# A four-layer attention and bilinear-MLP kernel whose instruction orders and PSUM banks are exchanged for another set

## The chip, the cores and the metric

The kernel runs on one core of one Trainium2 chip. The metric is the device time of one execution in microseconds (us), the median of several runs; lower is better. Engine names are those of the profile: PE is the matrix engine's matmuls, PEld its weight loads, DVE the vector engine, ACT the scalar engine, POOL the GpSimd engine, SP the SyncE queue that issues nearly all DMAs here.

## What is computed

Two sub-layers, A (sliding, dilated local attention) and B (a bilinear gated MLP), each behind a layernorm and with a residual, run twice on one sequence of 2048 tokens with 448 features.

```python
def _A_ref(x, wqkv, wo):              # H = 16 heads of 28
    W, dil = 8, 2                     # 8 keys, every second position back
    q, k, v = ...                     # x @ wqkv, split by heads
    idx = pos[:, None] - off[None, :]
    logits = jnp.einsum("bhsd,bhswd->bhsw", q, kg) * scale
    attn = _softmax(jnp.where(mask, logits, -1e9), axis=-1)
    o = jnp.einsum("bhsw,bhswd->bhsd", attn, vg)
    return o.reshape(B, S, D) @ wo
def _B_ref(x, w_gate, w_up, w_down):  # F = 1792
    return ((x @ w_gate) * (x @ w_up)) @ w_down
x = x + _A_ref(_layernorm(x), A_wqkv, A_wo)
x = x + _B_ref(_layernorm(x), B_w_gate, B_w_up, B_w_down)
x = x + _A_ref(_layernorm(x), A_wqkv, A_wo)
x = x + _B_ref(_layernorm(x), B_w_gate, B_w_up, B_w_down)
```

## The kernel before, in words

**Layers and chunks.** The layers are numbered 0 (A), 1 (B), 2 (A), 3 (B). Each is cut into chunks of 256 or 512 tokens, and the chunks of neighbouring layers are interleaved. The building code appends every piece of work to one list (`Sched.add`); its place in the list is its number, from 0 to 1669, and these numbers are how this document names operations. An operation is one or several instructions of one engine with the results it needs (`deps`) and, for matmuls, the PSUM banks it takes (`acquire`) and who frees them (`release`).

**An A chunk.** DVE and ACT compute the layernorm of each block of 128 tokens: statistics (L583, L585), the inverse deviation by Ln and Exp (L586, L588), the normalised block xn (L604). xn is transposed into xnT: for layer 0 by PE and a copy out of PSUM (L614, L618, L628), for the other layers by a DMA that transposes (L607), which is operation ("T", layer, block). Queries and keys are matmuls over WQK (halves of one unit on PE), copied to qk by ACT or DVE (L714). V is a matmul copied to v_sb by ACT or DVE (L806, L779); in layers 0 and 2 the last four heads of most query blocks take another way: spare columns of WQK make them beside the queries and keys, DMAs copy them to memory (L723, tile vt) and a transposing DMA, the reload, brings them back (L734, ("VT", layer, block)). Scores (L837) are bursts of small matmuls in 32-column tiles, and in the first six groups of layer 0 in 64-column tiles. Exp runs on ACT (L847), the mask on DVE (L854). The product with V (L872) is another burst; two copies to O_sb (L886, ACT or DVE) and an addition (L890) follow, then the division through Ln and Exp (L900 to L913), which leaves oT. In layer 2 small DMAs, the moves, regroup oT so that its fourth chunk is half as long (L445, oT<-oT; ("mv", ...) and after them ("mw", ...)); a like regrouping of wo_g is loaded once (("wf", ...)). The output projection takes oT and wo_g, and DVE adds it to x_sb (L943).

**A B chunk.** 14 units of 128 features each: 14 matmuls (seven pairs over the two halves of the rows of PE, L352) make gate and up; ACT copies gate to g_sb (L979), DVE multiplies it with up into hT (L982). The down projection then takes hT and WD, and DVE adds to x_sb. The blocks of the last layer go out by DMA.

**What sets the order.** The order on every engine is written out by hand as a list of numbers, `ORDER["pe"]`, `["act"]`, `["dve"]`, `["pool"]`, `["sp"]` (from L104). Where an operation may run on ACT, DVE or POOL, the list it stands in decides. An entry of PE like `801+802+785*848/6/1` is a merged burst: the small matmuls of 801, 802 and 785 are spread between steps of the unit 848, of which six steps run as eight strips of 32 columns each (L355); the last number says how many whole steps go ahead. `BANKS` gives each matmul operation its PSUM banks. `schedule` (L227) expands the lists, and derives the waits for banks from the order; `emit` (L276) writes each engine's instructions with semaphore waits for what has not been waited for yet. Each engine, and the DMA queue of SP, works its list strictly in order.

**Operations that the text speaks of.** 47 to 62 are warm-up matmuls without use for the result; 63 to 70 copy the loaded query and key weights into WQK (L522, by DVE, ACT or POOL); 71 to 78 copy the four heads' columns (L530); 45 and 46 write qmask (L509, L510); 211, 212, 271, 272, 532 and 533 are halves of the score bursts of the groups 0, 2 and 5 of layer 0. 279 and 280 are the two copies to O_sb of group 2; 245 is a copy of V, 373 a smaller one; 362, 512, 588 and 590 copy queries and keys. 301 and 303 are transposes for the first B chunk. 776 and 777 are reloads for the query blocks 1 and 2 of layer 2; 801, 802, 785 and 786 their bursts with V; 917 is a transpose for the second A chunk of layer 2, whose query/key units begin with 922 or 928; 819 loads a part of the regrouped wo_g, which 823 finishes and 824 uses. 1229 is the last move ahead of 1230, the first half of the output projection of the blocks 8 and 9 of layer 2. 855 to 890, 1037 to 1060 and 1254 to 1293 are gate/up units and their copies.

Of the kernel before, what the change touches and what calls it, by code (L numbers as in the profile page):

```python
# [96 lines left out]
def grp_nc(g):  # L97
# [22 lines left out]
    ),  # L120
    "act": (
# [1003 lines left out]
```

## Time and profile before

| what | value |
|---|---|
| runs | 383.13, 384.85, 381.83 us; median 383.13 |
| profiled execution, its own time | 383.47 us |
| its span, first to last instruction | 381.7 us |
| granted PE clock | 1.000 |
| instructions of PE | 6388 matmuls, 6388 weight loads |

The profile shows one execution. The span is what the trace covers; 1.8 us of the execution's own time lie around it. Busy time of PE is from the start of a matmul to a modelled end, and matmuls overlap: two that use different halves of the rows run side by side, so a step's real cost is read from the start of one to the start of the next. Line numbers are those of the kernel; L352 and L355 are helpers that nearly all matmuls share, so the tiles tell them apart. "Idle before <-releaser" names what the profile takes to have ended an engine's idle time; where the named one has nothing to do with the instruction, it was another.

### The profile page before, as it was taken

To read this page: it belongs to the slowest core of one execution; us is meant where nothing else is said; L and a number is where in the kernel's file an instruction comes from. 1 tells how busy PE (TensorE), PEld (TensorE's weight loads), DVE (VectorE), ACT (ScalarE), POOL (GpSimd) and SP (SyncE) were. 2 spreads that over 40 slices of the span, in tenths; PEclk is the share of its full clock that TensorE was granted. 3 is DMA by queue.
4 is the path that set the end of the run, shared out by engine and by line. 5 is a ranking of instruction groups with operands and counts; after the bars stand their busy time and mean duration, and the time that the engine had idled before them with its cause. 6 is when DMAs were issued, how large, how long until landed. Compare 5 with 4: busy or idle time off the path is not lost.

```text
span 381.7 us, 14424 instructions
## 1 busy us (share of the span) xinstructions
PE 373.9 (98%) x6388; PEld 209.8 (55%) x6388; DVE 288.1 (75%) x649; ACT 198.0 (52%) x379; POOL 7.8 (2%) x36
## 2 busy tenths in 40 slices
PE   7999999999999999999999999999989999999997
PEld 3645577654554445444676666555555544444864
DVE  7988999989759794968568977758887878266423
ACT  5798896766516355245645326628745633034410
POOL 7000000000000000000000000000000000000000
PEclk9999999999999999999999999999999999999999
DMA  7665543500130215332102221630124001502003
GB/s 262 165 158 147 96 127 81 97 7 3 26 78 16 43 25 72 43 43 44 34 18 27 45 50 29 106 47 6 25 43 76 9 19 29 122 17 47 2 2 120
DMA packets 56209, 22.97 MB, mean 60 GB/s; under 512 B 45812, under 2 KB 56132, under 8 KB 56148
## 3 DMA queue, kind: packets, MB, share of 16 engines
q1 hardware_dynamic: 56004, 22.00, 27.5%
q8 instruction: 50, 0.82, 0.9%
q14 instruction: 11, 0.09, 0.1%
q10 hardware_dynamic: 144, 0.06, 0.1%
HBM read 8.59 MB, written 2.71 MB: 30 GB/s over the span
## 4 chain that ended last, share of the span: by engine, by line
PE 91%; DVE 4%; ACT 2%; DMA 1%; issue 1%; SPq 0%; DVEq 0%
PE ps L352 82%; PE ps L355 4%; PE ps L837 2%; PE ps L872 2%; PE ps L994 1%; ACT qk L714 1%; DMA v_sb<-vt 1%; DVE xn_sb L604 1%; DVE st L583 1%; DMA x_sb<-in_A_x_dram 1%; DVE v_sb L806 0%; DVE WQK L522 0%; DVE hT L982 0%; DVE Qz L825 0%; DVE xnTa L628 0%
## 5 line engine op out<-in xcount | busy, mean ns | idle before, releaser
L352 PE MATMUL ps<-xnTb,WGU 64*128 64x512 bf16 (+1 forms) x1890 | 171.2, 332 | 0.3 <-DVE qk L714 0.3
L352 PEld LDWEIGHTS ps<-xnTb,WGU 64*128 64x128 bf16 x1890 | 92.3, 94 | 70.6 <-issue 1.6
L979 ACT ACTIVATE g_sb<-ps 128x512 bf16<-128x512 f32 (+1 forms) x140 | 69.3, 510 | 83.9 <-PE ps L352 72.0
L982 DVE TENSOR_TENSOR hT<-g_sb,ps 128x512 bf16<-128x512 bf16 (+1 forms) x140 | 78.0, 574 | 36.3 <-ACT g_sb L979 35.5
L352 PE MATMUL ps<-WD,hT 64*128 64x448 bf16 x794 | 81.3, 349 | 0.0
L352 PEld LDWEIGHTS ps<-WD,hT 64*128 64x128 bf16 x794 | 38.3, 94 | 33.3 <-ACT E_sb L847 0.4
L943 DVE TENSOR_TENSOR x_sb<-x_sb,ps 128x448 bf16<-128x448 bf16 x62 | 37.1, 613 | 21.6 <-PE ps L352 21.3
L352 PE MATMUL ps<-xnTa,WQK 64*128 64x512 bf16 (+1 forms) x490 | 51.8, 352 | 0.3 <-DVE WQK L522 0.2
L847 ACT ACTIVATE E_sb<-ps,shift_sb 128x1024 bf16<-128x1024 f32 (+1 forms) x36 | 37.5, 1072 | 12.0 <-PE ps L837 11.9
L583 DVE BATCH_NORM_STATS2 st<-x_sb 128x6 f32<-128x448 bf16 x64 | 38.3, 613 | 1.0 <-DMA x_sb<-in_A_x_dram 0.8
L604 DVE TENSOR_SCALAR xn_sb<-x_sb,mv,rstd 128x512 bf16<-128x512 bf16 (+1 forms) x64 | 35.4, 574 | 2.5 <-ACT rstd L588 2.0
L352 PEld LDWEIGHTS ps<-xnTa,WQK 64*128 64x128 bf16 x490 | 23.0, 94 | 20.7 <-DVE O_sb L890 0.4
L714 ACT ACTIVATE qk<-ps 128x1024 bf16<-128x1024 f32 (+1 forms) x29 | 26.6, 931 | 11.4 <-PE ps L352 6.3
L901 ACT ACTIVATE R_sb<-R_sb 128x480 f32<-128x480 f32 (+1 forms) x34 | 20.4, 604 | 17.2 <-DVE R_sb L900 17.0
L854 DVE TENSOR_TENSOR E_sb<-E_sb,MK 128x1024 bf16<-128x1024 bf16 (+1 forms) x36 | 23.5, 656 | 6.6 <-ACT E_sb L847 6.6
L352 PE MATMUL ps<-wo_g,oT 64*128 64x448 bf16 x236 | 27.1, 349 | 1.1 <-DVE hT L982 1.1
L913 DVE TENSOR_TENSOR oT<-O_sb,R_sb 128x480 bf16<-128x480 f32 (+3 forms) x36 | 21.9, 626 | 3.8 <-ACT R_sb L902 3.6
L352 PE MATMUL ps<-WV,xnTa 64*128 64x336 bf16 (+3 forms) x248 | 23.2, 304 | 0.5 <-DVE O_sb L890 0.5
L900 DVE STREAM_SHUFFLE R_sb<-O_sb 128x480 f32<-128x480 f32 (+1 forms) x34 | 23.1, 692 | 0.0
L586 ACT ACTIVATE lnv<-mv,eps_sb 128x2 f32<-128x2 f32 (+2 forms) x31 | 9.0, 295 | 25.9 <-DVE mv L585 24.0
L902 ACT ACTIVATE R_sb<-R_sb 128x480 f32<-128x480 f32 (+1 forms) x34 | 20.0, 607 | 0.3
L886 ACT ACTIVATE O_sb<-ps 128x512 f32<-128x512 f32 (+1 forms) x20 | 10.9, 570 | 15.8 <-PE ps L872 15.8
(66 smaller groups left out, 223.8 us busy)
## 6 DMA issues: line engine op xcount, KB each, us to landing
out_dram<-x_sb SPq DMA_DIRECT2D x15, 112.0 KB, 1.8
x_sb<-in_A_x_dram SPq DMA_DIRECT2D x3, 448.0 KB, 5.3
hT<-in_A_wqkv_dram SPq DMA_DIRECT2D x4, 224.0 KB, 4.4
WGU<-in_B_w_gate_dram SPq DMA_DIRECT2D x4, 224.0 KB, 3.9
WGU<-in_B_w_up_dram SPq DMA_DIRECT2D x4, 224.0 KB, 4.5
WD<-in_B_w_down_dram SPq DMA_DIRECT2D x2, 448.0 KB, 3.8
WGU<-in_B_w_gate_dram SPq DMA_DIRECT2D x2, 336.0 KB, 4.5
WGU<-in_B_w_up_dram SPq DMA_DIRECT2D x2, 336.0 KB, 4.8
```

The costliest lines, as they stand in the source:

```text
L352: return lambda E: E.matmul(out(), lhs(), rhs(), start=start, stop=stop)
L583: sc.add("dve", one(lambda E, B=B: E.bn_stats(st6[:, B, :], x_sb[:, B, :]), ("bn", li, B)), 525.0, deps=[("x", li - 1, B)] + ([("xn", li - ...
L604: sc.add("dve", one(lambda E, B=B, dst=dst, src=src: E.tensor_scalar(dst, src, mv[:, B, 0:1], rstd[:, B:B + 1], ALU.subtract, ALU.mult), ( ...
L714: return E.activation(dst, src, ACT.Copy) if hasattr(E, "activation") else E.tensor_copy(dst, src)
L847: return E.activation(E_sb[:, slot, 2 * hp:2 * hp + 2, 0:w], ps[:, b0:b0 + 2, 0:w], ACT.Exp, bias=shift_sb[:, 0:1], scale=SCALE)
L854: return E.tensor_tensor(e, e, MK[:, kind, 0:nc].unsqueeze(1).unsqueeze(1).to_broadcast([128, 2, w // nc, nc]), ALU.min)
L900: sc.add("dve", one(lambda E: E.stream_shuffle(R_sb[:, rs, 0:w], O_sb[:, os_, 0:w], [DH] * 32), ("Rs", li, qb)), dve_est(w) + 20.0, deps=[ ...
L901: sc.add("act", one(lambda E: E.activation(R_sb[:, rs, 0:w], R_sb[:, rs, 0:w], ACT.Ln), ("Rl", li, qb)), act_est(w, False), deps=[("Rs", l ...
L913: return E.tensor_tensor(oT[:, :, a % HALF:a % HALF + z - a], O[:, :, a - tok:z - tok], R_sb[:, rs, 0:w].rearrange("p (h n) -> p h n", h=4 ...
L943: sc.add("dve", one(lambda E: E.tensor_tensor(x_sb[:, B, :], x_sb[:, B, :], ps[:, bk[w], 0:D], ALU.add), ("x", li, B)), dve_est(D), deps=[ ...
L979: sc.add("act", one(lambda E, gs=gs, bk=bk: E.activation(g_sb[:, gs, 0:nt], ps[:, bk[0], 0:nt], ACT.Copy), ("G", li, j, fc)), act_est(nt), ...
L982: sc.add("dve", one(lambda E, gs=gs, bk=bk, fc=fc: E.tensor_tensor(hT[:, fc, hs, 0:nt], g_sb[:, gs, 0:nt], ps[:, bk[1], 0:nt], ALU.mult), ...
```

## The change

All five orders and the table of banks are replaced; nothing else in the file differs. The 1670 operations are the same, and so are their shapes and the data that each needs. The new lists were searched with every transpose, move, copy and reload assumed to land late, and the initial loads ("fetches") left as they were. By comparison of the lists: 42 operations change engine, so that ACT has 383 entries for 379 and DVE 588 for 592; 68 steps of merged bursts run as strips instead of 69; the first loads stand in the same order on SP. The score bursts 211/212, 271/272 and 532/533 stood directly behind each other, and now other matmuls stand between their halves. 45 and 46 move to the front of DVE's list, POOL copies 65 and 64 in the place of 67 and 64, and makes masks after them.

The core of the diff, with the lines that the text speaks of:

```diff
     "pe": (
-        "47 48 49 50 51 52 53 54 55 112 56 57 58 109 59 60 61 127 62 130 206 238 207 136 239 133 194 198 195 199 232 200 233 196 201 226 197 227 228 155 149 229 "
-        "230 158 152 231 171 189 211 212 356 192 174 357 180 354 247 248 177 355 502 217 218 503 352 253 353 585 581 254 582 586 504 506 242 505 507 243 266 371 "
-        "267 271 272 372 358 508 359 509 277 583 278 584 381 382 375 579 376 405 580 406 387 307 310 388 313 319 322 304 290 316 291 328 340 532 533 334 331 325 "
-        "337 343 400 521 401 411 522 412 346 526 347 527 348 538+539+556*349/5/1 424 598 425 599 454 451 448 557+562*457/2/5 463 563+609*551/2/2 552 466 610 460 "
...
-        "801+802+785+786*863/5/2 727 875 857 922 866 923 887 924 926 925 927 941 869 928 878 946 942 929 881 1019 947 1022 1028 952 953 860 1031 872 1040 1043 "
...
-        "1367+1368*1284/4/2 1287 1201 1396 1202 1356 1290 1357 1351 1230 1352 1231 1397+1373+1374*1293/7 1296 1304 1297 1305 1361 1402+1403*1306/4 1362 1298 "
-        "1425+1426*1299/4/3 1307 1479 1473 1482 1476 1431+1432*1485/7 1494 1488 1491 1500 1420 1391 1421 1392 1512 1497 1503 1506 1509 1515 1523 1524 1449 1525 "
...
+        "47 48 49 50 51 52 53 54 55 56 57 112 58 59 60 109 61 62 127 206 130 207 133 238 239 136 194 200 195 201 232 198 233 226 196 199 155 197 227 158 230 228 "
+        "149 152 229 231 211 171 212 189 356 174 192 357 177 180 354 247 248 355 502 217 218 503 352 253 353 581 254 585 582 586 242 506 504 243 505 507 266 271 "
+        "267 371 272 358 508 372 359 509 583 277 584 278 381 382 375 376 579 405 580 406 307 304 387 313 388 310 316 319 322 290 328 291 532 334 340 325 533 411 "
+        "331 412 343 400 337 401 521 526 522 346 347 527 348 538+539+556*349/5/1 424 598 425 599 454 451 562+557*448/3 457 551 563 552 463 469 609+610*475/2 460 "
...
+        "712 773 752 706 756 774 757 750 715 754 753 751 697 755 709 652 779 780 653 769 718 795+796*719/2/5 770 720 721 724 725 854 726 851 801+802+785*848/6/1 "
+        "786 727 863 857 875 869 866 928 887 929 926 922 927 924 923 925 946 881 941 947 952+953*942/3/1 878 1022 1019 860 1031 1034 1028 1040 872 824 981 "
+        "958+959*825/3 1052 884 1043 1025 982*890/1/3 891 1046 987+988*896/2/5 892 1037 893 1049 897 1055 898 1083 1058 899 1077 1080 1061 976 1062 1089 1092 "
...
+        "1206+1207*1120/1/6+1171/1 1121 1257 1254 1172 1122 1260 1266 1332 1269 1338 1183+1184+1212+1213*1333/4+1339/3 1272 1336 1334 1337 1335 1281 1263 "
+        "1367+1368*1278/4/3 1290 1275 1396 1201 1351 1202 1352 1284 1356 1287 1230 1357 1231 1397+1373+1374*1293/7 1304 1361 1296 1402+1403*1297/5/2 1362 1298 "
...
     "act": (
-        "14 106 107 102 103 118 119 110 113 124 125 131 68 208 137 209 240 202 241 204 237 146 147 205 203 186 168 234 187 169 150 235 153 236 213 214 193 362 "
-        "249 250 361 510 223 224 256 255 588 263 259 264 260 511 512 244 273 274 374 298 299 363 513 280 279 589 383 384 287 407 408 308 283 311 284 288 314 320 "
...
+        "14 106 107 102 103 118 113 119 110 124 125 66 131 208 134 209 137 240 241 202 146 147 205 237 156 204 203 234 168 169 186 187 150 235 213 214 236 178 "
+        "249 250 361 219 510 223 224 255 256 590 263 264 259 260 244 511 245 273 274 298 299 373 374 363 513 589 280 384 383 407 408 308 283 284 305 287 314 288 "
...
     "dve": (
-        "15 17 104 105 16 100 111 101 114 116 108 117 115 120 122 126 129 123 121 128 65 66 45 135 140 132 63 70 69 138 134 139 160 144 161 142 182 143 164 162 "
...
-        "221 222 252 360 225 257 262 258 590 265 261 270 245 268 269 294 373 295 296 297 275 276 302 380 300 281 404 286 385 377 587 282 386 531 409 309 312 285 "
...
+        "15 17 45 46 104 105 16 100 111 101 116 114 108 115 117 122 120 126 121 123 129 128 132 140 135 68 63 67 70 69 141 138 144 142 139 145 162 143 182 154 "
+        "163 148 160 164 166 157 165 184 159 151 167 161 210 183 185 179 173 188 170 153 72 76 73 74 172 77 191 190 176 175 193 246 181 362 215 216 270 251 220 "
+        "221 222 252 360 225 257 262 258 265 588 261 512 268 269 294 296 295 297 275 302 300 276 380 279 404 281 282 377 385 386 409 587 286 531 309 306 285 315 "
...
     "pool": (
-        "21 24 25 32 26 23 35 39 33 36 18 34 28 44 20 37 29 40 19 30 38 27 41 31 42 43 22 67 64 71 78 73"
+        "24 22 25 32 23 35 26 44 20 28 29 27 30 18 19 36 21 65 64 39 33 31 40 75 41 78 71 42 34 37 43 38"
...
     "sp": (
...
-        "379 378 519 524 99 595 525 529 597 594 596 530 593 441 443 591 445 592 447 606 601 602 671 673 669 607 675 743 749 745 747 843 767 845 764 768 766 762 "
-        "841 847 763 765 772 776 917 819 777 915 919 921 1016 1018 816 817 815 814 935 820 821 934 822 938 939 936 818 823 937 940 945 944 950 949 1076 1074 973 "
...
+        "378 519 518 379 99 593 595 591 529 594 596 443 525 441 447 592 445 597 530 607 602 606 601 671 673 675 669 745 749 743 747 845 843 766 768 820 762 765 "
+        "767 764 763 841 847 772 776 777 917 915 919 921 822 819 821 1018 1016 944 938 940 939 823 814 816 817 934 937 815 935 936 818 945 949 950 1140 1074 "
...
 BANKS = (
-        "47:0 109:1 112:2 127:45 130:23 133:23 136:01 149:01 152:45 155:45 158:01 171:45 174:01 177:67 180:45 189:23 192:23 194:01 196:45 198:67 200:01 206:67 "
...
+        "47:0 109:1 112:2 127:45 130:01 133:23 136:01 149:01 152:67 155:01 158:01 171:67 174:23 177:23 180:45 189:67 192:67 194:67 196:23 198:45 200:23 206:67 "
```

101 rows, old and new, of tables (BANKS, ORDER) are left out of this document.

## The prediction

> **What bounds the kernel now.** I read the page first, then the waits of PE, then the busy time by stretch, then the timeline at each place where PE waits. From the page, the span and the busy time by engine:
>
> ```profile
> span 381.7 us, 14424 instructions
> PE 373.9 (98%) x6388; PEld 209.8 (55%) x6388; DVE 288.1 (75%) x649; ACT 198.0 (52%) x379; POOL 7.8 (2%) x36
> ```
>
> PE is busy for 373.9 of 381.7 us, and no other engine passes 75%. So 7.8 us of PE idle time is all that another order can remove, and only orders change here. The waits of PE over the whole span say where it lies (total, times, longest):
>
> ```profile
> PE ps L514 <- DVE hT L475: 1.3, 1, 1.3
> PE ps L352 <- DVE hT L982: 1.1, 1, 1.1
> PE ps L614 <- DVE xn_sb L604: 0.7, 2, 0.4
> PE ps L872 <- DMA v_sb<-vt: 0.5, 1, 0.5
> PE ps L352 <- DVE O_sb L890: 0.5, 1, 0.5
> PE ps L618 <- DVE xn_sb L604: 0.5, 1, 0.5
> PE ps L352 <- DVE qk L714: 0.3, 1, 0.3
> ```
>
> L514, L614 and L618 belong to the start (warm-up and transposes); after it PE idles four times, 2.4 us in all. The stretches agree (us, then busy time of PE, PEld, DVE, ACT and POOL, the granted clock, DMA share, GB/s):
>
> ```profile
> 0.00:24.00 24.00, 21.09 (x288) 11.31 (x290) 21.68 (x76) 16.96 (x38) 7.82 (x36) 1.00 0.73 206
> 24.00:60.00 36.00, 35.17 (x780) 21.41 (x777) 32.14 (x75) 31.57 (x53) 0.00 (x0) 1.00 0.51 119
> ```
>
> 2.9 us are idle before 24 us, 0.8 between 24 and 60, and in this second stretch DVE is busy for 32.14 of 36 us.
>
> **The change part by part.** No operation is added or removed. The sum is made against the profiled execution's 383.47 us; the median of the runs shown is 383.13, 0.34 lower, and they spread over 3.0.
>
> *Reload at 162 us.* PE, then SyncE:
>
> ```profile
> 161.62 0.40 PE L355 MATMUL ps<-xnTb,WGU 64*32 64x512 bf16 x8
> 161.89 0.40 PE L355 MATMUL ps<-xnTb,WGU 64*32 64x512 bf16 x8
> 162.82 0.25 PE L872 MATMUL ps<-E_sb,v_sb 64*32 64x64 bf16 x16 [0.53 <-DMA v_sb<-vt]
> 162.89 0.40 PE L355 MATMUL ps<-xnTb,WGU 64*32 64x512 bf16 x8
> ```
> ```profile
> 157.47 1.26 SPq L607 DMA_TRANSPOSE xnTa<-xn_sb  x1
> 158.83 0.42 SPq L445 DMA_DIRECT2D wo_g<-in_A_wo_dram  x1
> 159.30 2.36 SPq L734 DMA_TRANSPOSE v_sb<-vt  x1
> ```
>
> One step of such a burst follows the other after 0.27 us (161.62 to 161.89); here it took 1.00, so 0.73 is lost. Operation 802 wanted reload 777, which SyncE issued at 159.30 and which PE had 3.5 us later. In the new SP order 777 stands straight behind 776, ahead of transpose 917 (1.26) and the load 819 (0.42): it goes out 1.7 us earlier. That covers 0.73: **-0.73** (bounds -0.73 and 0). Transpose 917 goes back by one reload, about 1.2 us; it feeds a query/key chunk that PE began (922) two gate/up units after the burst (875, 857) and now begins (928) after five (863, 857, 875, 869, 866), and the load 819 serves only 824, far behind that. I cost both at nothing; without that cover they cost what the reload takes, 1.3 us at most.
>
> *Move at 277 us.* PE, SyncE, DVE:
>
> ```profile
> 274.01 0.59 PE L352 MATMUL ps<-WV,xnTa 64*128 64x336 bf16 x6
> 274.44 1.67 PE L352 MATMUL ps<-xnTb,WGU 64*128 64x512 bf16 x14
> 275.95 1.16 PE L352 MATMUL ps<-WV,xnTa 64*128 64x336 bf16 x14
> 278.25 0.93 PE L352 MATMUL ps<-wo_g,oT 64*128 64x448 bf16 x8 [1.14 <-DVE hT L982]
> ```
> ```profile
> 274.73 0.54 SPq L445 DMA_DIRECT2D oT<-oT  x1
> ```
> ```profile
> 274.62 1.14 DVE L943 TENSOR_TENSOR x_sb<-x_sb,ps 128x448 bf16<-128x448 bf16 x2
> ```
>
> Three pairs of 64x336 take 274.01 to 274.44, 0.143 each; seven from 275.95 end at 276.95. The next matmul, 1230, starts at 278.25, so 1.3 us are lost. The profile names hT, but 1230 reads no hT: it needs the two PSUM banks that the x additions of 274.62 freed by 275.76, and the move 1229 (oT<-oT, 274.73). The move is what is left, 3.5 us from issue to use. In the new PE order, after the same scores burst, 1290, 1275, 1396, 1201, 1351, 1202, 1352, 1284, 1356 and 1287 stand ahead of 1230, before it was 1287, 1201, 1396, 1202, 1356, 1290, 1357, 1351: two more gate/up units of 1.51 us (274.44 to 275.95) with the V halves unchanged, some 3.0 us more cover for 1.3 us of lateness: **-1.3** (bounds -1.3 and 0). The Trainium skill, "DMA: Bandwidth & Descriptors", section "Anatomy of one DMA", puts a DMA's fixed cost at about 2.0 us (for issues from GpSimd). By that the move is there at 276.7 and the wait has another cause; the trace has 3.5 us from issue to use. By the Trainium skill's figure the sum would be without the -1.3, and it is a rival below.
>
> *The first 24 us.* DVE, PEld and POOL:
>
> ```profile
> 8.68 0.81 DVE L522 COPY WQK<-hT 128x448 bf16<-128x448 bf16 x2
> 9.43 0.63 DVE L604 TENSOR_SCALAR xn_sb<-x_sb,mv,rstd 128x512 bf16<-128x512 bf16 x1
> 10.83 0.64 DVE L522 COPY WQK<-hT 128x448 bf16<-128x448 bf16 x3
> 18.10 0.37 DVE L510 MEMSET qmask<- 28x1 f32 x4
> ```
> ```profile
> 8.69 1.22 POOL L522 COPY WQK<-hT 128x448 bf16<-128x448 bf16 x2 [1.92 <-DMA hT<-in_A_wqkv_dram]
> ```
> ```profile
> 21.22 0.41 PEld L618 LDWEIGHTS ps<-ident,xn_sb 64*128 64x128 bf16 x16 [0.44 <-DVE xn_sb L604]
> 22.11 0.14 PEld L837 LDWEIGHTS ps<-Qz,qk 64*64 64x64 bf16 x8 [0.28 <-DVE xnTa L628]
> ```
>
> Three copies alone take 0.64, two beside POOL's copies 0.81, so POOL holds DVE up by about 0.4 there. The new order still gives POOL two copies (65 and 64 for 67 and 64), but 65 can start with an earlier load; DVE runs five in one row. DVE's mask writes (0.37, from 18.10) go to the gap before the first input lands. I take **-0.7**, the 0.37 and half of the two waits of 0.28 and 0.44; bounds 0 (DVE is held up again) and -1.1 (0.37 and both waits). The 16 warm-up matmuls are the same number, two of them now fill the first wait for xn.
>
> *Split scores visits.* In the early groups the scores run in another array tiling, which PE enters and leaves:
>
> ```profile
> 38.08 0.92 PE L352 MATMUL ps<-wo_g,oT 64*128 64x448 bf16 x8
> 38.92 0.64 PE L837 MATMUL ps<-Qz,qk 64*64 64x128 bf16 x32
> 39.50 0.74 PE L352 MATMUL ps<-WV,xnTa 64*128 64x448 bf16 x6
> ```
> ```profile
> 47.46 0.42 PE L837 MATMUL ps<-Qz,qk 64*64 64x128 bf16 x16
> 47.81 0.61 PE L352 MATMUL ps<-xnTa,WQK 64*128 64x256 bf16 x8
> ```
>
> A visit of 32 holds the queue for 0.58 us, one of 16 for 0.35: two halves cost 0.12 more, and the entry about 0.08 (38.08 to 38.92, less four pairs of 0.19). The new order splits three visits (211/212, 271/272, 532/533): **+0.6**, bounds 0 and +0.8. Visits to the 32-column bursts stay at 32, strip steps go from 69 to 68, both nothing.
>
> *24 to 60 us.* Copies change engines. Groups by shape:
>
> ```profile
> L714 DVE CAST qk<-ps 128x1024 bf16<-128x1024 f32 x5 | 6.1, 1216 | 0.9 <-PE ps L352 0.9
> L806 DVE CAST v_sb<-ps 128x672 bf16<-128x672 f32 x7 | 6.0, 855 | 3.4 <-PE ps L352 2.8 <-ACT v_sb L779 0.6
> L886 DVE COPY O_sb<-ps 128x512 f32<-128x512 f32 x5 | 3.4, 680 | 0.9 <-PE ps L872 0.9
> ```
>
> To DVE come 362 and 512 (1.22 each) and 279 (0.68), off it go 245 (0.86) and a smaller V copy (373); 588 and 590 change places. That is about 2 us more in a stretch where it had 3.9 us idle and where PE waits for O_sb (0.5) and qk (0.3). On the other side 279 beside 280 halves the two O_sb copies that ACT ran one after the other ahead of the first of these waits. I take **0**, bounds -0.8 and +2.0. The later exchanges between ACT and DVE lie past 60 us, where PE's only waits are the two costed above; PE's work covers them, and without it each costs at most its own length, 1.2 us for the longest.
>
> Sum: 383.47 - 0.73 - 1.3 - 0.7 + 0.6 = **381.3 us**, 0.5% under the median. What is late next: the transposes into the first gate/up chunk (301, 303), near 49 us, and O_sb and qk there.
>
> **The rivals.**
> - *The wait at 277 us is not the move's* (something else that 3 us of other matmuls do not cover), so the change does not do there what it says. For it: the profile names DVE. Against: no operand or bank of 1230 fits. 381.3 + 1.3 = 382.6. Chance 0.12.
> - *DVE becomes the bound between 24 and 60 us* (the other side). DVE runs in order; with 2 us more of copies ahead of products and masks that free banks, PE waits for it. Bounded by the idle time that DVE has there, 3.9 us: 381.3 + 3.9 = 385.2. It decides from 2.2 us on, where the gain is eaten. For it: 32.14 of 36 us are busy and both early waits are DVE's. Against: ACT's copies go the other way. Chance 0.16; above 1% slower only if the stall carries on past 60 us, 0.07.
> - *All early waits go too*: 0.8 more between 24 and 60, 0.4 more at the start, and the splits cost nothing (0.6): 379.5. Against: DVE has more work there, not less. Chance 0.14, of which 0.10 below 379.3.
>
> **How the numbers follow.** The forecast, 381.3, has 0.58. Its own range, from the terms' bounds taken half each way, is 380.0 to 382.6. Together with half of what the second rival adds and the third, 379.3 to 384.3 leaves out 2 in 10. About 1% is what a measurement of this kernel tells from no change, 379.3 and 387.0 around the median. Faster by over 1%: 0.10. Slower by over 1%: 0.08, the second rival's tail and something unseen. Within 1%: 0.82.
>
> **What would show it.** In the changed kernel's waits of PE, the lines for v_sb<-vt and for hT before L352 are gone or under 0.3 us; PE's idle time before 24 us falls from 2.9 towards 2.2; the scores of the early groups show visits of 16 where they had 32; PE's idle time between 24 and 60 stays near 0.8. I am wrong if that last number exceeds 3, if a new DMA line of over 1 us appears among PE's waits, or if PE's busy time itself grows by more than 1 us.

## The result and the profile after

| | before | after |
|---|---|---|
| median, 20 runs each | 383.42 us | 381.88 us |
| lowest and highest | 381.83 to 385.12 | 381.46 to 383.43 |
| standard deviation of the 20 runs | 0.93 | 0.48 |
| profiled execution, span | 383.47, 381.7 | 381.83, 380.1 |

The ratio is 0.9965 (95% interval 0.9952 to 0.9978): 0.35% faster, and the runs lie closer together. The page of the changed kernel, span and busy time by engine:

```profile
span 380.1 us, 14424 instructions
PE 374.3 (98%) x6382; PEld 209.4 (55%) x6382; DVE 289.2 (76%) x645; ACT 198.7 (52%) x383; POOL 8.1 (2%) x36
```

Its waits of PE over the whole span:

```profile
PE ps L514 <- DVE hT L475: 1.3, 1, 1.3
PE ps L618 <- DVE xn_sb L604: 0.7, 1, 0.7
PE ps L352 <- DVE WQK L522: 0.4, 1, 0.4
PE ps L618 <- DVE xnTa L628: 0.3, 1, 0.3
PE ps L352 <- DVE qk L714: 0.2, 1, 0.2
```

The lines for v_sb<-vt, for hT ahead of L352 and for O_sb are gone, and no line of a DMA has come in their place; what is left lies in the first 24 us, but for 0.2. Busy time by stretch, columns as in the prediction: the two stretches shown there, then those around 162 and 277 us in the changed kernel, and the same two in the kernel before.

```profile
0.00:24.00 24.00, 21.28 (x288) 11.52 (x290) 21.65 (x75) 17.36 (x38) 8.13 (x36) 1.00 0.73 200
24.00:60.00 36.00, 35.73 (x776) 21.32 (x770) 33.35 (x74) 31.58 (x53) 0.00 (x0) 1.00 0.51 122
...
153.00:170.00 17.00, 17.00 (x292) 8.50 (x290) 12.46 (x33) 7.31 (x15) 0.00 (x0) 1.00 0.27 40
...
255.00:300.00 45.00, 44.94 (x1089) 24.32 (x1097) 37.31 (x78) 30.15 (x50) 0.00 (x0) 1.00 0.24 38
```
```profile
153.00:170.00 17.00, 16.47 (x282) 8.03 (x278) 13.36 (x34) 5.14 (x11) 0.00 (x0) 1.00 0.36 45
...
255.00:300.00 45.00, 43.84 (x1010) 24.87 (x1008) 37.02 (x78) 27.37 (x46) 0.00 (x0) 1.00 0.19 34
```

PE's idle time fell by 0.5 and 1.1 us around the two waits, by 0.6 (0.83 to 0.27) between 24 and 60 us, and by 0.2 (2.91 to 2.72) at the start.

Idle time is not yet time gained, because matmuls overlap and their ends are modelled. A firmer ledger needs no ends. At some places both orders have finished the same set of PE operations; the trace gives the start of the first matmul behind such a place, and the difference of two of them is what a stretch cost. (Two of the places, 72.1 and 293.4, lie inside a merged burst; the ends of these bursts give the same differences within 0.04 us.) By the profiled executions:

| stretch (us in the kernel before) | before | after | difference | forecast |
|---|---|---|---|---|
| start to 21.3 | 21.25 | 21.29 | +0.04 | -0.7 |
| 21.3 to 72.1 | 50.89 | 50.59 | -0.30 | +0.6 (splits) and 0 |
| 72.1 to 153.8 | 81.70 | 81.69 | -0.01 | 0 |
| 153.8 to 168.2 | 14.39 | 13.68 | -0.71 | -0.73 |
| 168.2 to 255.0 | 86.72 | 86.92 | +0.20 | 0 |
| 255.0 to 293.4 | 38.43 | 37.06 | -1.37 | -1.3 |
| 293.4 to 379.1, the last matmul | 85.71 | 85.87 | +0.16 | 0 |
| from there to the end of the span | 2.6 | 3.0 | +0.4 | 0 |

The sum is -1.6, as the spans say. The place near 277 us in the changed kernel, PE and then SyncE:

```profile
274.57 1.67 PE L352 MATMUL ps<-xnTb,WGU 64*128 64x512 bf16 x14
276.08 0.92 PE L352 MATMUL ps<-wo_g,oT 64*128 64x448 bf16 x8
```
```profile
272.19 0.55 SPq L445 DMA_DIRECT2D oT<-oT  x1
```

The unit of 274.57 runs its normal 1.51 us, and 1230 follows at once, 3.9 us behind the issue of move 1229.

### The profile page after: what moved, and what is told of

Same layout as the page of the kernel before. It is cut to its first block, busy times and chain, and to the rows that moved or that the text cites. A ratio compares the mean times of both kernels' runs of the same rounds, so it can differ in the third digit from the quotient of the medians.

```text
span 380.1 us, 14424 instructions
## 1 busy us (share of the span) xinstructions
PE 374.3 (98%) x6382; PEld 209.4 (55%) x6382; DVE 289.2 (76%) x645; ACT 198.7 (52%) x383; POOL 8.1 (2%) x36
## 4 chain that ended last, share of the span: by engine, by line
PE 91%; DVE 4%; DMA 2%; issue 1%; SPq 0%; ACT 0%; DVEq 0%
PE ps L352 83%; PE ps L355 3%; PE ps L837 2%; PE ps L872 2%; PE ps L994 1%; DMA xnTb<-xn_sb 1%; DMA x_sb<-in_A_x_dram 1%; DVE xn_sb L604 1%; DVE O_sb L886 1%; DVE E_sb L854 1%; DVE st L583 0%; DVE R_sb L900 0%; PE ps L618 0%; SPq L445 0%; DVE WQK L522 0%
## 5 line engine op out<-in xcount | busy, mean ns | idle before, releaser
L352 PE MATMUL ps<-xnTb,WGU 64*128 64x512 bf16 (+1 forms) x1898 | 172.4, 332 | 0.2 <-DVE qk L714 0.2
L352 PEld LDWEIGHTS ps<-xnTb,WGU 64*128 64x128 bf16 x1898 | 91.5, 94 | 71.0 <-DMA xnTb<-xn_sb 0.5
L352 PE MATMUL ps<-WD,hT 64*128 64x448 bf16 x798 | 81.9, 349 | 0.0
L352 PEld LDWEIGHTS ps<-WD,hT 64*128 64x128 bf16 x798 | 38.5, 94 | 33.0 <-DVE hT L982 0.4
L352 PE MATMUL ps<-xnTa,WQK 64*128 64x512 bf16 (+1 forms) x490 | 52.2, 352 | 0.4 <-DVE WQK L522 0.4
L352 PEld LDWEIGHTS ps<-xnTa,WQK 64*128 64x128 bf16 x490 | 23.1, 94 | 21.0 <-DVE hT L982 0.6
L352 PE MATMUL ps<-wo_g,oT 64*128 64x448 bf16 x230 | 26.9, 349 | 0.0
L714 ACT ACTIVATE qk<-ps 128x1024 bf16<-128x1024 f32 (+1 forms) x24 | 21.2, 917 | 10.4 <-PE ps L352 10.3
L352 PE MATMUL ps<-WV,xnTa 64*128 64x336 bf16 (+3 forms) x244 | 22.9, 305 | 0.1
L872 PEld LDWEIGHTS ps<-E_sb,v_sb 64*32 64x32 bf16 x1088 | 13.4, 90 | 7.3 <-issue 1.6
```

The costliest lines, as they stand in the source:

```text
L352: return lambda E: E.matmul(out(), lhs(), rhs(), start=start, stop=stop)
L714: return E.activation(dst, src, ACT.Copy) if hasattr(E, "activation") else E.tensor_copy(dst, src)
L872: parts[eb // 2].append((lambda E, b=b, c=c, o=o, vw=vw, eb=eb, eo=eo: E.matmul(ps[32 * b:32 * b + 32, bk[c], o:o + nc], vw, E_sb[64 * c:6 ...
```

## The experiments

Edits are shown as the numbers in an engine's list; everything else of the kernel named stays as it is. "Ratio" is to the kernel before on the same chip.

**What did 1230 wait for near 277 us?** In the kernel before, DVE's product 1292, which the profile had named, goes behind the two statistics 1453 and 1454.

```diff
 "dve"
-1455 1358 1292 1453 1454
+1455 1358 1453 1454 1292
```

> The kernel before with one edit on DVE: the product 1292 (hT, which the profile names as what ended PE's wait of 1.1 us at 277 us) goes behind 1453 and 1454. Theory (the wait is for the move 1229): matmul 1230 starts some 3.5 us after the move's issue, as before, and before or apart from the end of 1292, which comes 0.6 to 0.7 us later. Rival (it is DVE's product, as the profile says): 1230 starts 0.05 us after the end of 1292, 0.6 to 0.7 us later than before.

One run: 383.87 us. DVE, PE and SyncE:

```profile
278.42 0.18 DVE L585 BATCH_NORM_AGGREGATE mv<-st 128x2 f32<-128x6 f32 x1
278.52 0.65 DVE L982 TENSOR_TENSOR hT<-g_sb,ps 128x512 bf16<-128x512 bf16 x1
```
```profile
278.66 0.93 PE L352 MATMUL ps<-wo_g,oT 64*128 64x448 bf16 x8 [1.31 <-DVE mv L585]
```
```profile
274.99 0.54 SPq L445 DMA_DIRECT2D oT<-oT  x1
```

1230 started 0.51 us before the product ended (278.52 + 0.65 = 279.17), so it did not wait for it; the wait is still 1.31 and now carries the name of a statistic, which 1230 does not read either. What has kept its distance is the move: 3.67 us from issue to use, 3.52 in the profile before. In the last experiment below the profile names the move itself (0.22 <-DMA oT<-oT). The first rival is out.

**The reload alone**, in the kernel before:

```diff
 "sp"
-776 917 819 777 915
+776 777 917 819 915
```

> The kernel before with one edit on SyncE: reload 777 straight behind 776, ahead of transpose 917 and load 819. Theory (the queue order made the reload late): PE's wait of 0.7 us at 162 us is gone, the later matmuls come 0.7 us earlier, nothing else changes, time 382.7 against 383.4. Rival (917 or 819, now later by 1.2 us, make PE wait instead, or the reload is slowed by what it now shares the DMA engines with): the wait shrinks by less than half or comes back before 200 us, time 383.4.

382.82 us, ratio 0.9987 (0.9976 to 0.9999). The wait at 162 us is gone, and PE is 0.68 ahead behind the burst; but at the query chunk 922, six microseconds on, this row stands:

```profile
168.02 0.82 PE L352 MATMUL ps<-xnTa,WQK 64*128 64x512 bf16 x6 [0.24 <-DMA xnTa<-xn_sb]
```

There 0.21 is left of the 0.68. Of the four transposes that 922 needs only 917 was passed; the last one, 921, stands behind the same DMAs in both lists. It landed at 167.89 here and at 167.57 in the kernel before, so it is above all PE that comes too soon for it, since 922 is only two gate/up units behind the burst in the old PE order. The prediction looked for this cost at transpose 917, and took it as nothing because the new PE order has five units there; without that cover most of the gain is lost.

The same run shows something of more weight. Its PE and SP orders around 277 us are those of before, and yet:

```profile
275.83 1.16 PE L352 MATMUL ps<-WV,xnTa 64*128 64x336 bf16 x14
276.83 0.92 PE L352 MATMUL ps<-wo_g,oT 64*128 64x448 bf16 x8
```
```profile
274.62 0.54 SPq L445 DMA_DIRECT2D oT<-oT  x1
```

No wait: the same move was there at most 2.2 us after its issue. **Where such a DMA lands differs from execution to execution.** The prediction had set 3.5 us from the trace against the about 2.0 us of fixed cost that the Trainium skill gives for issues from GpSimd ("DMA: Bandwidth & Descriptors", section "Anatomy of one DMA"). Both turn up here for one and the same move: at most 2.2 in this run and in the one with 279 on DVE below, 3.52 and 3.67 in two others.

The traces hold what makes the difference, though the views above do not print it: the time of every semaphore update that a DMA sends as its parts land (16 for move 1229), and the packets of the queue that the profile calls "instruction". In the kernel before, 15 of the 16 updates came by 276.73 and the last at 278.11, 0.14 us ahead of 1230. One instruction packet of 16 KB ran from 275.62 to 277.02; the DMA view from 275 to 278 us lists it (packets, MB, share):

```profile
q8 instruction: 1, 0.02, 2.9%
```

With DVE's product late the last update came at 278.52, again 0.14 us ahead of 1230, and again 1.10 behind the end of an instruction packet. In the run with the reload moved no packet was near, and all 16 had come by 276.54. Twelve traces (all but the two with landings made late, below) hold 96 such last moves. The 60 with no instruction packet between 0.3 and 1.9 us after their issue landed 1.70 to 2.29 us after it; all 28 that took longer than 2.3 us, up to 3.79, had one (8 had one and were not late). That the packet causes the lateness is read from this coincidence; no run moves the one without the other.

**The move alone**, the other way round: in the changed kernel 1230 goes back ahead of the two gate/up units.

```diff
 "pe"
-1202 1352 1284 1356 1287 1230 1357
+1202 1352 1230 1284 1356 1287 1357
```

> The changed kernel with 1230 moved forward again, ahead of the units 1284 and 1287 and the V half 1356 (3.4 us of matmuls). In the changed kernel 1230 starts 3.88 us after the issue of its move 1229. Theory (the move needs about 3.5 us, and the cover of matmuls is what hid it): 1230 now waits for some 3.0 us, part of which later work cannot give back, time 383.5 to 385. Rival (the wait was not the move's): PE finds 1230 ready, time 381.9.

385.78 us, ratio 1.0065 (1.0042 to 1.0088). PE, DVE, and a stretch of the windows:

```profile
274.69 1.13 PE L352 MATMUL ps<-wo_g,oT 64*128 64x448 bf16 x8 [1.97 <-DVE x_sb L943]
275.62 3.20 PE L352 MATMUL ps<-xnTb,WGU 64*128 64x512 bf16 x14
278.60 0.65 PE L352 MATMUL ps<-WV,xnTa 64*128 64x336 bf16 x6
```
```profile
274.04 0.60 DVE L943 TENSOR_TENSOR x_sb<-x_sb,ps 128x448 bf16<-128x448 bf16 x1
```
```profile
250.00:300.00 50.00, 47.80 (x1042) 24.98 (x1040) 37.87 (x80) 29.85 (x50) 0.00 (x0) 0.97 0.20 36
```

A wait of 1.97 came, and it is a bank's: the x addition that frees it ends at 274.64, PE starts at 274.69, 2.5 us behind the move. So the units moved ahead cover the addition too, and the run doesn't price the move by itself. The second half of the loss was foreseen by no one: the next 14 matmuls took 2.98 us (275.62 to 278.60) in place of 1.51. The clock record has 0.5 for 3.413 us there, from 275.29 on; 0.97 is its mean over the 50 us.

**Both waits taken out of the kernel before**, with a cover for 922:

```diff
 "sp"
-776 917 819 777 915
+776 777 917 819 915
 "pe"
-875 857 922 866 923
+875 857 866 922 923
-1357 1351 1230 1352 1231
+1357 1351 1352 1230 1231
```

> The kernel before with the two dear waits alone taken away: SyncE issues reload 777 straight behind 776, one more gate/up unit (866) stands ahead of query chunk 922 so that the transposes put back by the reload are covered, and one more gate/up unit (1352) stands ahead of projection 1230. Nothing else moves: no split visits, no new copies on DVE, the head and the tail of before. Theory (the two waits carry the gain, and the rest of the change sums to about nothing: head -0.35, 24 to 60 us -0.9, split visits and other PE work +0.9, tail +0.4): about 2.0 us under the kernel before, 381.1 to 381.5. Rival (a wait removed late in the program is given back before the end, as the reload's was when it was moved alone, and the gain needs the head and the stretch to 60 us): 382.2 to 382.8.

383.32 us, ratio 0.9998 (0.9979 to 1.0016), which is the rival's side and even short of it. In its profile both stretches are shorter, 13.72 and 37.61, and other stretches, which the edit does not touch, are longer. That made a second table worthwhile: what the stretches took in every profiled execution (us; [e] where the edit lies in the stretch or ahead of its uses).

| stretch | before | DVE product late | reload | 279 on DVE | both waits | after | tail | masks | joined forward |
|---|---|---|---|---|---|---|---|---|---|
| start to 21.3 | 21.25 | 20.74 | 21.25 | 20.67 | 21.87 | 21.29 | 20.98 | 20.95 [e] | 20.84 |
| 72.1 to 77.1 | 4.91 | 4.96 | 4.93 | 5.83 | 5.42 | 5.02 | 5.02 | 5.02 | 5.06 |
| 153.8 to 168.2 | 14.39 | 14.40 | 14.16 [e] | 14.03 | 13.72 [e] | 13.68 | 13.68 | 13.68 | 13.68 |
| 215.8 to 255.0 | 39.20 | 39.81 | 39.21 | 40.09 | 39.62 | 39.44 | 39.46 | 39.42 | 39.46 |
| 255.0 to 293.4 | 38.43 | 38.59 [e] | 37.50 | 37.84 | 37.61 [e] | 37.06 | 37.06 | 37.05 | 37.12 |

With the order of before, the last four stretches, where no edit touches them, vary by 0.4 to 0.9 us from one execution to the next, by waits in other places (for xnTb, the reload, a move). With the new order the last four rows repeat within 0.07; the one later stretch of it that does vary is 293.4 to 319.4 us (26.16, 26.44, 26.12 and 26.08), where the kernel with the other tail has a wait of 0.3 for a transpose. The start varies in both.

**One copy to O_sb moved**, in the kernel before (279 from ACT to DVE, as the changed kernel has it), to find what shortened the stretch from 24 to 60 us:

```diff
 "act"
-280 279 589
+280 589
 "dve"
-380 300 281 404
+380 300 279 281 404
```

> The kernel before with one copy of an attention output (279) taken from ACT to DVE, where the changed kernel has it: its fellow 280 stays on ACT, so that the two run side by side where ACT ran them one after the other. Theory (this is what shortened the stretch from 24 to 60 us by 0.9 us where nothing was forecast): PE's 0.5 us wait for O_sb near 45 us goes or falls under 0.15, 0.4 to 0.5 us by 60 us, 382.6 to 382.8 in all. Rival (the copy is not what that wait hung on, or DVE's extra 0.68 us delays another copy by as much): the wait for O_sb, or one in its place, stays at 0.4 or more, 383.0 to 383.4.

383.40 us, ratio 0.9999 (0.9979 to 1.0019). DVE and PE:

```profile
43.14 0.85 DVE L825 TENSOR_SCALAR Qz<-qk,qmask 128x960 bf16<-128x960 bf16 x2
43.91 0.73 DVE L604 TENSOR_SCALAR xn_sb<-x_sb,mv,rstd 128x896 bf16<-128x896 bf16 x1
44.56 0.68 DVE L886 COPY O_sb<-ps 128x512 f32<-128x512 f32 x1
```
```profile
45.55 0.60 PE L352 MATMUL ps<-WV,xnTa 64*128 64x336 bf16 x6 [0.61 <-DVE O_sb L890]
```

The rival holds: DVE comes to the copy only after two other operations, so the wait stays. Which of the exchanges removed it in the changed kernel was not tried.

**The split score visits joined again**, in the changed kernel, first by pushing the first halves back, then by drawing the second halves forward:

```diff
 "pe", pushed back
-231 211 171 212 189
+231 171 211 212 189
-266 271 267 371 272 358
+266 267 371 271 272 358
-532 334 340 325 533 411
+334 340 325 532 533 411
 "pe", drawn forward
-231 211 171 212 189
+231 211 212 171 189
-266 271 267 371 272 358
+266 271 272 267 371 358
-532 334 340 325 533 411
+532 533 334 340 325 411
```

> The changed kernel with the score halves 211/212, 271/272 and 532/533 behind each other again (171, 267 with 371, and 334, 340, 325 stand ahead of them). Theory (each split visit costs 0.2 us of PE): the PE time up to 60 us falls by 0.6, time about 381.3. Rival (what a joined visit saves comes back as a wait for the bank or the masks behind it): PE's idle time up to 60 us grows by what the visits save, time 381.9.

> The kernel after with the three split scores visits joined again by drawing the second half forward (211 212 together, 271 272 together, 532 533 together), where the earlier try pushed the first half back and so held up ACT's and DVE's lists. Theory (each split costs what the rows of the visits say, 0.12 for two halves and 0.08 for the entry): 0.4 to 0.6 us faster than the kernel after, 381.3 to 381.5, visits of 32 matmuls in place of 16, no new wait. Rival (the second half needs a bank or an operand that is not ready so early, or the units behind it now come late for ACT and DVE, so that a wait takes the gain): 381.9 or more, with a line of over 0.5 us among PE's waits before 65 us.

386.97 us, ratio 1.0097 (1.0070 to 1.0125), and 384.80 us, ratio 1.0040 (1.0024 to 1.0056). All three visits were joined at once. Both ways lose, by two lines among the waits of PE, pushed back and drawn forward:

```profile
PE ps L837 <- ACT E_sb L847: 1.2, 1, 1.2
PE ps L352 <- ACT E_sb L847: 1.0, 1, 1.0
```
```profile
PE ps L837 <- ACT E_sb L847: 1.4, 1, 1.4
...
PE ps L352 <- DVE E_sb L854: 0.5, 1, 0.5
```

The Exp on ACT empties the banks of the scores. When the scores come later, ACT and all that stands behind the Exp in its list wait; when they come earlier, PE waits for the Exp of the visit ahead. So the splits are not a cost to be had back: they stand where ACT has a bank free. Part of the loss of the kernel pushed back is the clock: in its profiled execution 3.413 us at a granted clock of 0.5 follow from 65.25 us on, by estimate half of that, 1.7 us, lost.

**The tail**, in the changed kernel: outputs whose data are ready early go ahead of the last burst.

```diff
 "sp"
-1618 1522 1616 1528 1600 1309 1124 1520 1530 1598 1606 1663 1311 1608 1669
+1618 1522 1616 1309 1124 1520 1530 1311 1528 1600 1598 1606 1608 1663 1669
```

> The changed kernel with the last outputs of SyncE's list put in the order in which their data come (1309, 1124, 1520, 1530 and 1311 ahead of 1528, 1600, 1598). In the changed kernel the last output is issued 0.21 us after its data (DVE ends at 377.78, issue 377.99), 0.03 before the change, because SyncE issues ten outputs back to back. Theory (the queue of outputs holds the last one up): the last issue follows its data by 0.03 us and lands sooner, the span after the last matmul shrinks by 0.2 to 0.4 us, time 381.5 to 381.7. Rival (the landing itself takes longer, whatever the order): the span after the last matmul stays at 3.0 us, time 381.9.

381.47 us, ratio 0.9958 (0.9941 to 0.9974). SyncE and DVE at the end, the changed kernel and then this one:

```profile
376.98 1.46 SPq L445 DMA_DIRECT2D out_dram<-x_sb  x3
```
```profile
377.39 0.39 DVE L998 TENSOR_TENSOR x_sb<-x_sb,ps 128x224 bf16<-128x224 bf16 x1 [0.95 <-PE ps L994]
```
```profile
377.75 0.33 SPq L445 DMA_DIRECT2D out_dram<-x_sb  x1
```
```profile
377.33 0.39 DVE L998 TENSOR_TENSOR x_sb<-x_sb,ps 128x224 bf16<-128x224 bf16 x1 [0.95 <-PE ps L994]
```

In the changed kernel the last output is the third of the row at 376.98, issued at 377.99, 0.21 after its data (377.39 + 0.39): ten outputs stand back to back ahead of it. With this edit it goes out 0.03 after them, and the span behind the start of the last matmul falls from 3.0 to 2.7 us. This is the fastest kernel measured, but its ratio's interval overlaps that of the changed kernel.

**POOL's masks ahead of its copies**, in the changed kernel:

```diff
 "pool"
-36 21 65 64 39 33 31 40 75 41 78 71 42 34 37 43 38
+36 21 39 33 31 40 41 42 34 37 43 38 65 64 75 78 71
```

> The changed kernel with POOL's ten mask operations ahead of its two weight copies, where POOL idles for 3.8 us. In the changed kernel POOL makes masks from 10.2 us on, beside DVE's five weight copies, which follow each other after 0.23 to 0.31 us where before they did after 0.19. Theory (POOL's work slows DVE's copies beside it): the copies follow each other after 0.19 us, the fifth ends 0.2 to 0.3 us sooner, PE's wait of 0.4 us for WQK shrinks by as much, time 381.6. Rival (the copies are slow for another reason, such as ACT's copy or the loads that still land): no change in them, time 381.9.

381.57 us, ratio 0.9963 (0.9948 to 0.9978). DVE's five copies, changed kernel and this one:

```profile
10.27 1.26 DVE L522 COPY WQK<-hT 128x448 bf16<-128x448 bf16 x5
```
```profile
10.19 1.00 DVE L522 COPY WQK<-hT 128x448 bf16<-128x448 bf16 x5
```

Without masks on POOL beside them the copies take 0.26 less. The start to 21.3 us is 0.34 shorter, but that of the kernel with the other tail, with nothing changed there, is 0.31 shorter: no gain can be told from the variation of the start.

**Landings made late on purpose**: in both kernels SyncE issues one more small load ahead of each transpose, reload and last move (83 in all); no result depends on them.

```diff
+                        if e == "sp" and (op.dma[:3] in ("d_t", "d_v") or op.dma[:3] == "d_m" and op.mode == 1):
+                            self.extra(E).then_inc(sems["d_more"], 16)
                         i = (fn or op.ins[n][0])(E)
...
+        return E.dma_start(more[:, k, :], A_x[0][0:128, 4 * k:4 * k + 4])
```

> The kernel before with one more small load (128 x 4 values into a tile that nothing reads) issued by SyncE ahead of each transpose (layers 1 to 3), each reload and each last move: 83 loads, none of which changes the result. Each puts off what stands behind it by some 0.45 us (SyncE's time for a small load) and a row of four transposes by up to 1.8. In the trace of before seven uses come less than 0.5 us after the landing they need, and three moves are used 2.4 to 3.5 us after issue. Theory (before had no margin for late landings): 3 to 10 us longer, 386 to 393. Rival (the margins do not matter, the later work absorbs it): 383 to 385.

> The changed kernel with the same 83 loads. In its trace one use comes less than 0.5 us after its landing, all others 1.3 us or more. Theory (the new order has the margin that it was searched for): 0 to 2.5 us longer, 382 to 384.4, and less than half of what the kernel before loses. Rival (the gain came from single places, not from margin): it loses as much as the kernel before, 3 us or more.

414.82 us, ratio 1.0808 (1.0772 to 1.0845), and 392.07 us (four runs, 389.46 to 396.05), ratio 1.0206 (1.0170 to 1.0243, worked out without the longest of the four). The waits of PE, before's order and then the new one (the added lines shift the numbers: L354 is L352, L357 is L355, L883 is L872):

```profile
PE ps L354 <- DMA xnTb<-xn_sb: 13.4, 6, 4.3
PE ps L883 <- DMA v_sb<-vt: 5.9, 5, 3.2
```
```profile
PE ps L883 <- DMA v_sb<-vt: 2.7, 2, 2.4
PE ps L357 <- issue: 2.2, 1, 2.2
...
PE ps L354 <- DMA xnTa<-xn_sb: 1.1, 1, 1.1
```

The old order loses some 32 us (414.82 against 383.10 on that chip), the new one 9 to 10 (390.90 without its longest run, 392.07 with it, against its 381.88 in the first measurement). The direction is that of the theory, both sizes are far above what was expected; phases of the halved clock are in both (mean clock 0.983 and 0.991).

**All close uses covered by hand**, in the kernel before, on top of the two edits of "both waits":

```diff
 "sp"
-443 591 445 592 447
+443 591 445 447 592
 "pe"
-1064 1005 1092 1006
+1064 1092 1005 1006
-1089 976 1101 977
+1089 1101 976 977
-1254 1257 1269 1266 1260 1121 1122
+1121 1254 1257 1269 1266 1260 1122
-1231 1397+1373+1374*1293/7 1296 1304
+1231 1296 1397+1373+1374*1293/7 1304
```

> The kernel before with more work put ahead of each use that came close behind a transpose, a reload or a move, or that waited in any of the profiled executions with the order of before: the two edits that took away the waits at 162 and 277 us alone, and beside them transpose 447 issued ahead of move 592, gate/up unit 1092 ahead of projection 1005, gate/up unit 1101 ahead of projection 976, the down units 1121 ahead of 1254 and 1296 ahead of the burst of 1293. The head, the stretch from 24 to 60 us, the split visits and the tail are those of before. Theory (where those DMAs land differs between executions of one order, each execution of before loses at another few of these uses, and the change gains by covering them all): against the mean of five profiled executions with the order of before the stretches fall from 5.2 to 4.9-5.0 (72 to 77 us), 14.3 to 13.7 (154 to 168), 35.4 to 35.0-35.1 (220 to 255) and 38.1 to 37.1-37.3 (255 to 293), 381.2 to 382.0 in all, and the spread between runs (standard deviation 0.9 before, 0.5 in the changed kernel) falls to 0.6 or less. Rival (covering these uses brings nothing that lasts, as the two waits alone brought nothing to the median: the gain hangs on something else in the new order): 382.9 to 383.6, spread 0.8 or more.

385.07 us, ratio 1.0041 (1.0027 to 1.0056). The runs lie close together (384.54 to 385.32, six of them), but 1.9 us above the kernel before:

```profile
278.87 1.73 PE L352 MATMUL ps<-wo_g,oT 64*128 64x448 bf16 x14 [0.22 <-DMA oT<-oT]
281.91 1.31 PE L352 MATMUL ps<-WD,hT 64*128 64x448 bf16 x12 [1.31 <-DVE x_sb L943]
```

Two stretches did what the theory said (72 to 77 us 4.90, 154 to 168 us 13.72), and two are longer than in the kernel before (216 to 255 us 40.11, where the run with 279 on DVE has 40.09 without an edit, and 255 to 293 us 39.52). In the last one a unit drawn forward needs a bank that an x addition has not freed yet: 1296 waits 1.31 us. The theory's time fell; of its spread only this much can be said, that six runs are few.

## Why the prediction was right, and where it was not

The forecast of 381.3 us is 0.6 under the measured median, and its "within 1%" is what came. One of its sums does not come out: the terms' bounds as stated, taken half each way, give 380.4 to 383.8 and not 380.0 to 382.6; the measured median lies in both. By its steps:

- *Reload at 162 us*, -0.73: measured -0.71. Right, and the cover was needed: moved alone the reload gives back 0.47 of 0.68 at 922. Its size too is one execution's: in the run with 279 on DVE the old order took 14.03 there, so 0.35 of it remains.
- *Move at 277 us*, -1.3: measured -1.37 between the two profiled executions. The cause is right (the product is excluded, the move's last update comes 0.14 us ahead of 1230 in two executions, and the move is named in the last run), but the size is one execution's. In two of the four profiled executions with the old PE order there 1230 did not wait at all. A price read from one profile was taken as a property of the order.
- *The first 24 us*, -0.7: this failed. PE passes 21.3 us at the same time (+0.04), and idle time before 24 us fell by 0.2. The forecast was the 0.37 of DVE's mask writes, which did move to the front, and half of two waits. PE's waits only changed places: the two for xn ahead of L614 went (0.7), one for DVE's copies into WQK (0.4) and one for xnTa (0.3) came, and POOL's masks run beside these copies (1.26 us where 1.00 are to be had). The start varies by 1.2 us between executions of the old order anyway; the means of the unedited ones in the second table are 21.16 and 21.04.
- *Split scores visits*, +0.6: too much. Rows of the changed kernel:

```profile
37.53 0.42 PE L837 MATMUL ps<-Qz,qk 64*64 64x128 bf16 x16
37.88 0.93 PE L352 MATMUL ps<-wo_g,oT 64*128 64x448 bf16 x8
```

  A half holds the queue for 0.35, as forecast, but by the ledger the stretch with the first two splits (36.7 to 41.6 us) grew by 0.20, 0.10 for each, and that with the third (55.8 to 67.8) not at all. And they were taken for a pure cost, where the joined variants show that they keep PE from waiting for ACT.
- *24 to 60 us*, 0: idle time fell from 0.83 to 0.27 although DVE's busy time rose from 32.14 to 33.35. The wait for O_sb went (41.6 to 46.0 us: 4.45 to 3.87), and the 9.8 us behind it grew by 0.23. So the second rival, DVE as the bound, did not come; the third came in this one part only.
- What was missing: +0.4 at the tail, where outputs queue ahead of the last one and 0.4 in small pieces after 168 us.

That the sum came so near is in part luck. Against the profiled executions the errors leave 0.5 us: 0.7 too much gain at the start and 0.8 of losses missing later, against 0.9 too little gain between 21 and 72 us.

The deeper reason is better told by the spread than by the sum. The profile before showed two DMA waits of 1.7 us together; other executions of the same order have waits of a like total in other places. By the second table, unedited executions of the old order against the four of the new one, the means of its last four rows fall by 0.18, 0.59, 0.14 and 0.85, 1.8 us together, where the one pair of profiles has 1.7 in them with other shares (+0.11, -0.71, +0.24, -1.37). The new order leaves nearly all of these waits out, which is why its stretches repeat. It is not that its DMAs land early: in its profiled execution four of the eight last moves landed 2.7 to 3.7 us after issue (in that of the kernel before only one took that long), and PE waits for none of the eight.

That this alone accounts for the 1.5 us between the medians is argued and not shown. With the two waits out by themselves the table would give some 0.9 us (14.27 to 13.72, and 37.92 to 37.61), and the median did not move; the interval of that run ends at -0.8. The covers by hand made new waits and so decide nothing. Which of the new lists, beside SP's and PE's at these two places, the gain needs stays open.

## What to carry to other kernels

A wait for a DMA in one profile is a draw: look at how short the way from issue to use is everywhere, and at several executions, before pricing one. In lists that each engine works strictly in order, moving one unit ahead as cover also moves its need for a bank ahead, so the visits drawn forward and the set of covers made here by hand cost more than they saved; check who frees the bank as well as who brings the data. An output queue at the end should hold nothing that could have gone out earlier.

## What the runs showed of the hardware

- One and the same move between tiles of SBUF took at most 2.2 us from issue to use in two executions and 3.52 and 3.67 us in two others, with the same instructions around it. In twelve traces the last moves without an instruction packet between 0.3 and 1.9 us after issue all landed within 2.29 us; the 28 of 96 that took longer than 2.3 us all had one.
- A wait of 1.97 us of PE was followed by a granted clock of 0.5 for 3.413 us in the profiled execution of that kernel, and by their mean clock (0.995 or 0.996) in four more of its six runs; the sixth, with the clock at 1.000, took 384.13 us where the others took 385.65 to 386.80. The length of a wait alone does not decide it: 1.22 us with two short ones behind it were enough in the kernel pushed back, while 1.3 us (before) and 1.4 (drawn forward), and even 2.93 us in one piece (the kernel before with late landings, at 264 us), were not. What does is told by windows: the slow phases of one trace start whole multiples of 3.413 us apart (78.49, 174.07 and 320.84: 28 and 43 of them). Twelve traces have a slow phase to cut them into such windows by. From the start of the clock record to the last matmul, all eight windows in which PE idled 1.56 us or more (by the modelled ends) were followed by the halved clock, and none of those with 1.51 us or less; the 2.93 us fell into two windows. The Trainium skill, "TensorE: Matmul & The Clock Gate", Part 1, has the half rate come after at least one idle window of about 3.4 us, in a window that runs freely: the length of the slow phase agrees, and so does the free-running window, but about 1.5 us of idle time in one window were enough here.
- With POOL's masks beside them DVE's five copies took 1.26 or 1.27 us in five traces, without them 1.00 in the one trace of that edit.
